# Memory attention and gated MLP: two issue loops and a hand-placed start replaced by one list of steps with named PSUM banks

## The chip, the cores and the metric

The kernel runs on one core of one Trainium2 chip. The metric is the device time of one execution in microseconds (us). The core has five instruction queues that run side by side and each in its own order: TensorE (PE, with its weight loads as PEld), VectorE (DVE), ScalarE (ACT), GpSimd (POOL) and SyncE (SP, which here issues every DMA). They wait for each other through semaphores. SBUF is the on-chip memory that all work on, PSUM the 8 banks of 128 x 512 float32 into which PE writes.

## The reference, cut to what matters

```python
B, H, S, D = (4, 8, 576, 64)
scores = scale * np.matmul(q, k.transpose(0, 1, 3, 2))      # causal mask, softmax over the last axis: a
local = np.matmul(a, v)
q_p = phi(q)                                                 # where(x > 0, x, exp(x) - 1) + 1
mem_ret = np.einsum('bhsd,bhde->bhse', q_p, M_prev)
mem_norm = np.einsum('bhsd,bhd->bhs', q_p, z_prev)[..., None] + 1e-06
x = g * mem_ret / mem_norm + (1 - g) * local                 # g = sigmoid(beta), one per head
x = x.transpose(0, 2, 1, 3).reshape(2304, 512)
out = ((x @ w_a) * (x @ w_b)) @ w_out                        # d_ff = 1536; weights are float64
```

## The kernel before, in words

**Attention.** Two heads of one batch are worked together as a pair, so there are 16 pairs. For each pair PE transposes keys and queries (steps `TK`, `TQ`, and `Tq` for the 64 rows of the tail), ACT copies them to SBUF (`th…`) and DVE makes what the copy rounded off (`tl…`), since every product is made of three products of high and low parts. PE adds the mask (`b_…`) and the scores (`S_…`), DVE takes the minima of the negated scores (`m…`), ACT the exponentials (`e…`), DVE the reciprocals of the sums (`r_`), POOL multiplies the probabilities by them (`n0` to `n4`), PE transposes them (`G…`), ACT and DVE copy them (`h…`, `l…`, group 0 by POOL with `w_`, `l0`), and PE multiplies by the values (`V…`). The result of a pair goes to DRAM (`st_`) and comes back for the memory part (`pa` to `py`), which for the first two blocks of tokens runs inside the attention too. The tail's scores (`S_4`) and the values' product (`V…`) use one PSUM tile of two banks in turn; the six other banks are handed out by `psum()` in rotation.

**What sets the order.** The table `ORDER` names each step once with a lag. A loop over 19 rounds issues in each round the steps of the table in that order, each for pair (round minus lag). Ahead of it the first loads, the mask, the identity matrix and 17 products of zeros on PE (`warm(17)`) are written out by hand; 12 more products of zeros, the zeroing of the memory matrices and the gates stand after round 0. POOL's first work is written as: zero both `qdiag` tiles, scale the first one after its load (`sq(0)`), then make the identity.

**MLP.** The tokens are six blocks t of 384, d_ff is twelve parts f of 128. A column is one (t, f): twelve products with w_a (called A here), twelve with w_b (B), then ACT copies B out of PSUM (`cx`, L852), DVE multiplies it by A (`mx`, L855), ACT rounds that (`hh`, L859) and DVE takes the rest (`hl`), and nine products with w_out add it into the output's banks (`outer`, L877). `column(t, f)` issues A, B, the four steps, and then `outer` of the column before. In the first 18 columns A and B take their banks from a pool of two. The column order is: t = 0 and 1 in turn for f = 0 to 5, then t = 0 for f = 6 to 11, then t = 1, then blocks 2 to 5.

**Weights.** They come as float64 and are turned into float32 by whole-number steps, in 24 units, two for each f: a large one (w_a and w_b, 1024 columns) and a small one (w_out, 512). A unit goes through `mag` (ACT, L760), `clamp` (POOL, L766), `shift`, `high`, `low` (DVE, L773, L780, L787), `hi` (ACT, L802) and `lo` (DVE). The first three units start inside the attention; the generator `conversion()` does the others, one or two behind each column by the table `UNITS`.

**Memory part of blocks 2 to 5.** `memory_unit` has the steps load, phi, norm, turn, retrieve (PE, L1012, into one PSUM bank) and join (DVE, L1019, then ACT and DVE for the halves). The tables `E2` and `R2` say at which column those of block 2 stand; `retrieve` is issued between A and B of its column, for block 2 twice in one column at the end (`R2 = (20, 21, 23, 23)`).

## Time and profile before

| what | value |
|---|---|
| median of three runs | 698.15 us (696.22 to 699.35) |
| the profiled execution, its time | 697.51 us |
| the profiled execution, span from first to last instruction | 695.6 us |
| PE busy | 669.8 us (96%) |
| DVE, ACT, POOL busy | 446.8, 319.4, 243.9 us |
| mean granted clock of TensorE | 0.993 |

The profiled execution lies 0.64 us under the median. Its time is 1.9 us longer than its span, which is what lies around the instructions. A busy share is an average over stages: the attention fills about the first 200 us, the columns with the weight conversion reach to about 330 us, and from 380 us on PE runs columns alone.

### The profile page before, as it was taken

What the parts mean: (1) busy time and instruction counts of PE and PEld (TensorE: products, weight loads), DVE (VectorE), ACT (ScalarE), POOL (GpSimd) and SP (SyncE); (2) the same over time, 40 slices, a digit from 0 to 9 for tenths busy, and PEclk for the clock granted to TensorE, in tenths of its full rate; (3) what the DMA queues carried; (4) which work ended last, traced back from release to release, by engine and by line L of the source; (5) the groups of instructions that cost most, each with busy time, mean ns of one, the idle gap of its engine ahead of it and who ended that gap; (6) DMA issues with size and microseconds to landing.
All of it is one profiled execution on the core that took longest, in us unless ns stands there. A gap on an engine that the chain in (4) does not pass through costs nothing.

```text
span 695.6 us, 11360 instructions
## 1 busy us (share of the span) xinstructions
PE 669.8 (96%) x4125; PEld 615.8 (89%) x4125; DVE 446.8 (64%) x901; ACT 319.4 (46%) x765; POOL 243.9 (35%) x354
## 2 busy tenths in 40 slices
PE   7999999999979999989988999999999999999997
PEld 6798888999879898878988999999999999999996
DVE  4999998988878887887776544545445545421111
ACT  2999999999875445443322322222212321221111
POOL 4699999999893232232501100001000000000000
PEclk9999999999999999999999999999999999999999
DMA  8666647456733435441413311112110400010001
GB/s 169 143 146 170 155 125 206 118 150 198 248 135 129 158 121 164 156 134 17 124 40 69 92 34 29 33 51 64 35 35 0 112 15 23 1 46 1 0 1 45
DMA packets 124663, 64.24 MB, mean 92 GB/s; under 512 B 97856, under 2 KB 116288, under 8 KB 124608
## 3 DMA queue, kind: packets, MB, share of 16 engines
q1 hardware_dynamic: 124608, 63.53, 33.7%
q8 instruction: 32, 0.52, 0.3%
q14 instruction: 23, 0.19, 0.1%
HBM read 49.35 MB, written 14.16 MB: 91 GB/s over the span
## 4 chain that ended last, share of the span: by engine, by line
PE 77%; DVE 13%; ACT 4%; issue 3%; DMA 1%; SPq 1%; POOL 0%; ACTq 0%; DVEq 0%; POOLq 0%
PE pp L840 35%; PE o L877 17%; PE pt L87 8%; PE pt L442 6%; PE pw L611 6%; DVE wt L787 2%; DVE wt L780 2%; ACT wh L802 2%; PE pw L442 2%; PE m L1012 1%; DVE PT L91 1%; DVE wt L773 1%; DVE x L855 1%; DVE nm L481 1%; DVE wl L91 1%
## 5 line engine op out<-in xcount | busy, mean ns | idle before, releaser
L840 PE MATMUL pp<-xh,wh 128*128 128x384 f32 x568 | 193.6, 341 | 6.7 <-ACT x L852 3.9
L840 PE MATMUL pp<-xh,wl 128*128 128x384 f32 x568 | 192.1, 338 | 0.6 <-DVE wl L91 0.6
L840 PE MATMUL pp<-xl,wh 128*128 128x384 f32 x568 | 191.6, 337 | 0.0
L840 PEld LDWEIGHTS pp<-xh,wh 128*128 128x128 f32 x568 | 107.5, 189 | 13.4 <-ACT x L852 6.7
L855 DVE TENSOR_TENSOR x<-pp,x 128x384 f32<-128x384 f32 x71 | 39.4, 555 | 124.0 <-ACT x L852 124.0
L840 PEld LDWEIGHTS pp<-xl,wh 128*128 128x128 f32 x568 | 107.7, 190 | 2.8
L840 PEld LDWEIGHTS pp<-xh,wl 128*128 128x128 f32 x568 | 107.5, 189 | 1.0 <-DVE wl L91 1.0
L852 ACT ACTIVATE x<-pp 128x384 f32<-128x384 f32 x71 | 34.5, 487 | 146.1 <-PE pp L840 146.1
L1004 POOL TENSOR_TENSOR xx<-xx 128x384 f32<-128x384 f32 x16 | 16.5, 1036 | 204.1 <-DMA xx<-xs 199.0
L511 POOL TENSOR_SCALAR P<-P,sum 128x128 f32<-128x128 f32 (+2 forms) x144 | 82.8, 596 | 12.1 <-DVE sum L503 9.6
L877 PE MATMUL o<-wh,hl 128*128 128x512 f32 x216 | 85.5, 396 | 0.0
L877 PE MATMUL o<-wl,hh 128*128 128x512 f32 x216 | 85.0, 393 | 0.0
L877 PE MATMUL o<-wh,hh 128*128 128x512 f32 x216 | 84.9, 393 | 0.0
L492 ACT ACTIVATE P<-pt,nm 128x512 f32<-128x512 f32 (+3 forms) x128 | 66.6, 531 | 6.3 <-DVE nm L481 5.8
L91 DVE TENSOR_TENSOR PT<-pt,PT 128x512 fp32r<-128x512 f32 (+2 forms) x112 | 61.7, 587 | 10.0 <-ACT PT L566 7.8
L91 DVE TENSOR_TENSOR hl<-x,hh 128x384 fp32r<-128x384 f32 x71 | 40.5, 571 | 42.0 <-ACT hh L859 42.0
L859 ACT ACTIVATE hh<-x 128x384 fp32r<-128x384 f32 x72 | 37.8, 525 | 62.3 <-DVE x L855 62.3
L611 PE MATMUL pw<-PT,vh 128*128 128x320 f32 (+4 forms) x416 | 61.4, 293 | 3.0 <-issue 2.2
L611 PEld LDWEIGHTS pw<-PT,vh 128*128 128x128 f32 x416 | 57.1, 189 | 5.3 <-POOL xh L249 2.4
L481 DVE TENSOR_REDUCE nm<-pt 128x1 f32<-128x512 f32 (+3 forms) x128 | 56.3, 482 | 8.4 <-PE pt L442 8.2
L766 POOL TENSOR_SCALAR wt<-wt 128x512 f32<-128x512 f32 (+1 forms) x21 | 30.2, 1439 | 74.3 <-ACT wt L760 74.2
L87 PE MATMUL pt<-ident,P 128*128 128x128 f32 (+1 forms) x400 | 52.4, 279 | 1.5 <-POOL P L511 1.2
(126 smaller groups left out, 1079.8 us busy)
## 6 DMA issues: line engine op xcount, KB each, us to landing
xs<-xo SPq DMA_DIRECT2D x16, 576.0 KB, 4.3
xx<-xs SPq DMA_DIRECT2D x48, 192.0 KB, 3.4
wr<-in_moe_w_a_dram SPq DMA_DIRECT2D x12, 512.0 KB, 3.7
wr<-in_moe_w_b_dram SPq DMA_DIRECT2D x12, 512.0 KB, 4.8
wr<-in_moe_w_out_dram SPq DMA_DIRECT2D x12, 512.0 KB, 3.3
out_dram<-ob SPq DMA_DIRECT2D x18, 256.0 KB, 2.1
qr<-in_q_dram SPq DMA_DIRECT2D x34, 128.0 KB, 3.5
kr<-in_k_dram SPq DMA_DIRECT2D x32, 128.0 KB, 4.1
```

What stands on the lines that cost most here:

```text
L87: nc.tensor.transpose(out, x, ident[0:x.shape[0], 0:x.shape[0]])
L91: eng.tensor_tensor(out=lo, in0=x, in1=hi, op=ALU.subtract)
L442: nc.tensor.matmul(o, lhsT=w, rhs=x, start=first, stop=True, skip_group_check=True)
L481: nc.vector.tensor_reduce(out=s["nm"][:, c:c + 1], in_=src, axis=AX.X, op=ALU.min)
L492: nc.scalar.activation(out=s["P", i][:, h, :], in_=src, func=AF.Exp, scale=-1.0, bias=s["nm"][:, c:c + 1], accum_out=s["sum"][:, c:c + 1],)
L511: nc.gpsimd.tensor_scalar(out=pr[:, h, :], in0=pr[:, h, :], scalar1=r[:, c:c + 1], scalar2=1.0, op0=ALU.mult, op1=ALU.mult,)
L611: nc.tensor.matmul(pv[:, a:hi], lhsT=w, rhs=x, start=(n == 0), stop=(n == len(ops) - 1))
L840: nc.tensor.matmul(pp, lhsT=w[:, w0:w0 + P], rhs=x[:, kk, :], start=(c == 0), stop=(c == 3 * KK - 1),)
L852: nc.scalar.activation(out=x, in_=ps[1], func=AF.Copy)
L855: nc.vector.tensor_tensor(out=h[0], in0=ps[0], in1=h[0], op=ALU.mult)
L859: nc.scalar.activation(out=h[1], in_=h[0], func=AF.Copy)
L877: nc.tensor.matmul(po[t, m], lhsT=hx[:, m * P:(m + 1) * P], rhs=w[:, w0:w0 + DM], start=(f == 0 and n == 0), stop=(f == NFT - 1 and n == 2),)
```

## The change

The loop over `ORDER`, the text ahead of it, `conversion()` with `UNITS`, and the first 30 columns with their memory units are replaced by one list. `schedule()` yields a name and a pair (or column, or unit) at a time: `HEAD` and `TAIL` are written out step by step, `LOOP` holds two tables with lags for the rounds 3 to 8 and 9 to 13. Steps that were one are now several: the four steps of a column, its A (`uA`) and B (`uB`), its `outer` (`uo`) and the writing of finished outputs (`ua`, `ub`, `uc`) each have a name; so has every step of a weight unit (`Kload`, `Kmag`, … `Klo`), the load of a unit, and the memory unit's steps, with phi, norm, turn and join cut into two or three. What each step computes is unchanged. The attention's six PSUM banks are no longer handed out in rotation: each `psum()` takes the next number of a list, `BANKS`. Columns 30 to 71 and their memory units keep the old loop.

```diff
-ORDER = """
-clamp0:2 h3A:3 b_3:1 hi1:4 l3A:3 pd:2 S_3:1 pe:3 m3B:1 e4:2 v_l:2 TK:0 TQ:0 mc:1 m3A:1 mag2:3
...
+HEAD = """
+Dk.0 id.0 zi.0 ib.0 wm.17 wm.12 TK.0 Dq.0 Dk.1 TQ.0 zq.0 zq.1 thK.0 thQ.0 mk.0 Ek.1 TK.1 thK.1 b_2.0
...
+BANKS = """
+0123450123453140253102432540324015324103502313502143501234253134251034215305431305412305143240313240
...
+LOOP = """
+H1:2 hh:4 pd:2 pe:3 shift1:3 TQ:0 py:4 h3A:3 me:3 clamp1:3 l3A:3 mx:3 e4:2 LM:2 b_3:1 thQ:0 px:4
...
+TAIL = """
+h3A.11 pe.11 pf.11 b_3.13 pb.12 S_3.13 l3A.11 v_l.12 TK.14 m3B.13 e4.12 px.10 e3B.13 m3A.13 fw.0
...
+def schedule():
...
+    yield from named(HEAD)
+    lags = {}
+    for k, text in enumerate(LOOP.split("/")):
+        names = [w.partition(":") for w in text.split()]
+        lags |= {nm: int(o) for nm, _, o in names if o}
+        for i in range(SPAN[k], SPAN[k + 1]):
+            for nm, *_ in names:
+                if i >= lags[nm]:
+                    yield nm, i - lags[nm]
+    yield from named(TAIL)
...
-        ps_t = late.enter_context(tc.tile_pool(name="ps_t", bufs=6, space=bass.MemoryType.PSUM))
+        ps_t = late.enter_context(tc.tile_pool(name="ps_t", bufs=1, space=bass.MemoryType.PSUM))
...
+        banks = iter("".join(BANKS.split()))
+
         def psum():
-            return ps_t.tile([P, 512], F32, tag="T", name="pt")
+            return ps_t.tile([P, 512], F32, tag="T" + next(banks), name="pt")
...
-        for i in range(NPAIR + max(lags.values())):
-            for nm, o in lags.items():
-                p = i - o
-                if nm in KINDS or 0 <= p < NPAIR:
-                    step[nm](p)
-                if p == NPAIR - 1 and nm in after:
-                    after[nm]()
-            if i == 0:
-                warm(12)
-                memory_store(mem)
-                gates()
+        step |= beyond
+        for nm, p in schedule():
+            step[nm](p)
...
+    def hidden(c, n):
+        t, f = columns[c]
+        key, tag = "ab", "ab"
...
+        cols[c][0][n] = half(t, f, n, pools[key].tile([P, DM], F32, tag=tag, name="pp"))
+
+    def done(c):
+        t, f = columns[c]
+        outer(t, f, cols[c][1][1:])
...
+            "uA": lambda c: hidden(c, 0),
+            "uB": lambda c: hidden(c, 1),
+            "uo": done,
...
+        for c in range(CUT, len(columns)):
+            column(c, lambda: memory(c, True))
```

**The start.** These are POOL's first instructions behind its constants, before and then after. `qdiag` is the tile that holds the queries' tail rows, `ident` the matrix against which PE transposes, `mask_f` the causal mask.

```order
L277 MEMSET qdiag_101 128x512
L277 MEMSET qdiag_102 128x512
L358 ISA
L358 TENSOR_SCALAR qdiag_101<-qdiag_101 128x512
masks.py:197 MEMSET ident 128x128
masks.py:199 AFFINE_SELECT ident<-ident 128x128
masks.py:29 MEMSET mask_f 128x128
```

```order
masks.py:197 MEMSET ident 128x128
masks.py:199 ISA
masks.py:199 AFFINE_SELECT ident<-ident 128x128
L739 MEMSET qdiag_101 128x512
L739 MEMSET qdiag_102 128x512
masks.py:29 MEMSET mask_f 128x128
masks.py:30 AFFINE_SELECT mask_f<-mask_f 128x128
L451 TENSOR_SCALAR qdiag_101<-qdiag_101 128x512
```

The identity moves from behind the scaling of `qdiag`, which waits for a load, to POOL's first place. PE's first instructions, again before and then after (`idle` is the tile of zeros, `kr` and `qr` are keys and queries, `f` their transposed halves):

```order
L294 MATMUL pt<-idle 128x256 x17
L87 MATMUL pt<-ident,kr 128x128 x4
L87 MATMUL pt<-ident,qr 128x128 x4
L87 MATMUL pt<-ident,kt 128x128
L87 MATMUL pt<-ident,qdiag_101 128x128
L294 MATMUL pt<-idle 128x256 x12
```

```order
L387 MATMUL pt<-idle 128x256 x29
L187 MATMUL pt<-ident,kr 128x128 x4
L187 MATMUL pt<-ident,qr 128x128 x4
L187 MATMUL pt<-ident,kr 128x128 x4
L535 LDWEIGHTS ident_b
```

The second group of products of zeros now stands ahead of the first transposes, and the keys of the second pair are transposed before the first scores.

**The conversion beside the columns.** These are ACT's instructions at the columns 12 and 13, before and then after. `x<-pp` is a column's `cx`, `hh<-x` its `hh`, `wh<-wt` a weight unit's `hi`, `wt<-wr` its `mag`.

```order
L852 ACTIVATE x<-pp 128x384
L859 ACTIVATE hh<-x 128x384
L802 ACTIVATE wh_4409<-wt 128x512
L760 ACTIVATE wt<-wr 128x512
L802 ACTIVATE wh_4474<-wt 128x1024
L760 ACTIVATE wt<-wr 128x1024
L852 ACTIVATE x<-pp 128x384
L859 ACTIVATE hh<-x 128x384
```

```order
L921 ACTIVATE x<-pp 128x384
L928 ACTIVATE hh<-x 128x384
L893 ACTIVATE wh_4408<-wt 128x512
L853 ACTIVATE wt<-wr 128x512
L921 ACTIVATE x<-pp 128x384
L893 ACTIVATE wh_4489<-wt 128x1024
L853 ACTIVATE wt<-wr 128x1024
L928 ACTIVATE hh<-x 128x384
```

The copy of column 13 stood behind two units' steps and now stands behind one; the large unit's two steps come after it.

**The memory units of block 2.** These are DVE's instructions around the first `join`, before and then after. `xx<-m` is the join, which empties the bank of a `retrieve`; the rows ahead of it are phi and norm of a later unit, `q<-ph` with STREAM_TRANSPOSE is a turn.

```order
L966 TENSOR_SCALAR ph<-ph 128x384
L969 SCALAR_TENSOR_TENSOR ph<-q_4870,ph 128x384
L977 TENSOR_TENSOR q_4870<-ph,z_4703 128x384
L985 TENSOR_REDUCE n_4931<-q_4870 128x12
L988 COPY n_4933<-n_4931 32x12 x4
L989 TENSOR_TENSOR n_4932<-n_4931,n_4933 128x12
L990 TENSOR_SCALAR n_4932<-n_4932,over_gate_64 128x12
L994 RECIPROCAL n_4932<-n_4932 128x12
L995 TENSOR_TENSOR ph<-ph,n_4932 128x384
L1019 TENSOR_TENSOR xx<-m,xx 128x384
L91 TENSOR_TENSOR xl_69<-xx,xh_68 128x384
L855 TENSOR_TENSOR x<-pp,x 128x384
```

```order
L1079 RECIPROCAL n_4896<-n_4896 128x12
L1084 TENSOR_TENSOR ph<-ph,n_4896 128x384
L1115 TENSOR_TENSOR xx<-m,xx 128x384
L191 TENSOR_TENSOR hl<-x,hh 128x384
L1090 STREAM_TRANSPOSE q_4826<-ph 128x384
L924 TENSOR_TENSOR x<-pp,x 128x384
L1049 TENSOR_SCALAR ph<-ph 128x384
L1052 SCALAR_TENSOR_TENSOR ph<-q_4834,ph 128x384
L191 TENSOR_TENSOR xl_69<-xx,xh_68 128x384
```

Before, the join of unit 0 stands behind phi and norm of unit 2; now it stands ahead of them, behind those of unit 1. On PE there were B of column 20, an `outer` and A of column 21 between the `retrieve` of unit 0 and that of unit 1; now B of the columns 20 and 21, A of column 20 and an `outer` stand there, and the last two units' `retrieve`, which followed each other in one column, have an A between them. From column 4 on `outer` also stands a column later than it did: A and B of column 4 follow those of column 3 with no `outer` between them, `outer` of column 2 comes behind them, and so on until two of them stand behind column 14.

## Rows read from the trace of the kernel before

**Rows 1.** Busy time by stage: stretch, PE, PEld, DVE, ACT, POOL, clock.

```profile
40.00:180.00 140.00, 139.84 (x1216) 124.94 (x1216) 128.82 (x281) 129.38 (x373) 132.77 (x214) 1.00 0.62 161
180.00:217.48 37.48, 32.43 (x259) 30.36 (x258) 31.76 (x60) 27.34 (x71) 29.35 (x44) 1.00 0.45 152
217.48:327.82 110.34, 104.37 (x528) 94.81 (x528) 87.84 (x116) 51.55 (x76) 32.55 (x24) 0.98 0.42 136
327.82:380.00 52.18, 47.61 (x240) 44.13 (x241) 39.10 (x83) 13.83 (x28) 11.03 (x14) 0.97 0.32 76
```

**Rows 2.** The same view of the three stretches at half clock.

```profile
24.50:27.80 3.30, 3.30 (x23) 3.08 (x22) 3.22 (x8) 3.12 (x13) 3.30 (x6) 0.50 0.94 207
...
307.90:311.10 3.20, 3.20 (x11) 3.20 (x11) 3.13 (x5) 1.12 (x2) 1.24 (x1) 0.50 0.43 155
359.10:362.30 3.20, 3.20 (x11) 3.20 (x12) 2.08 (x4) 1.29 (x4) 0.00 (x0) 0.50 0.29 69
```

**Rows 3.** Start, in order of time: start, duration, instruction, idle time before it.

```profile
1.19 4.00 PE L294 MATMUL pt<-idle 128*128 128x256 f32 x17 [1.19 <-DVE idle L283]
...
7.16 0.62 POOL L358 TENSOR_SCALAR qdiag<-qdiag 128x512 f32<-128x512 f32 x1 [5.44 <-DMA qdiag<-in_q_dram]
...
8.35 1.12 PE L87 MATMUL pt<-ident,kr 128*128 128x128 f32 x4 [3.17 <-POOL ident masks.py:199]
...
10.40 2.91 PE L294 MATMUL pt<-idle 128*128 128x256 f32 x12
...
13.48 0.80 PE L442 MATMUL pt<-f 64*128 64x512 f32 x2
```

**Rows 4.** PE's longest wait while the pipeline fills, in order of time.

```profile
23.91 0.38 PE L442 MATMUL pt<-mask,ident_b 128*128 128x128 bf16 x4 [1.73 <-ACT P L492]
```

**Rows 5.** PE at the end of the attention, in order of time.

```profile
200.23 1.83 PE L611 MATMUL pw<-PT,vh 128*128 128x256 f32 x13 [2.23 <-issue]
...
205.86 3.35 PE L87 MATMUL pt<-ident,P 128*128 128x128 f32 x25 [1.20 <-POOL P L511]
```

**Rows 6.** ACT ahead of the first of these waits.

```profile
197.74 1.18 ACT L760 ACTIVATE wt<-wr 128x1024 f32<-128x1024 f32 x1
...
199.25 0.79 ACT L492 ACTIVATE P<-pw,nm 128x576 f32<-128x576 f32 x1
```

**Rows 7.** The chain that ended last, around column 14: start, duration, work.

```profile
305.02 1.14 ACT wt L760
...
306.58 6.00 PE pp L840 x24
312.59 2.09 PE o L877 x9
314.68 4.19 PE pp L840 x24
```

**Rows 8.** PE's first product of columns 12 and 14, in order of time.

```profile
289.65 0.44 PE L840 MATMUL pp<-xh,wh 128*128 128x384 f32 x1 [0.67 <-ACT x L852]
...
306.58 0.44 PE L840 MATMUL pp<-xh,wh 128*128 128x384 f32 x1 [3.28 <-ACT x L852]
```

**Rows 9.** Groups by form, 217 to 328 us: busy, mean ns, idle before.

```profile
L91 DVE TENSOR_TENSOR hl<-x,hh 128x384 fp32r<-128x384 f32 x16 | 8.9, 559 | 9.5 <-ACT hh L859 9.5
```

**Rows 10.** The weight units' tile, 217 to 330 us: POOL's clamp, ns min/median/max.

```profile
L766 POOL TENSOR_SCALAR wt<-wt x21: 616/1442/1546, 219.7 to 322.6; 128x512 f32<-128x512 f32 x11, 128x1024 f32<-128x1024 f32 x10
```

**Rows 11.** The memory units of block 2, in order of time.

```profile
358.23 0.55 DVE L1019 TENSOR_TENSOR xx<-m,xx 128x384 f32<-128x384 f32 x1
...
358.92 0.60 PE L1012 MATMUL m<-yh,md 128*128 128x384 f32 x1 [2.16 <-DVE xx L1019]
...
376.10 0.41 PE L1012 MATMUL m<-yh,md 128*128 128x384 f32 x1 [1.76 <-DVE xx L1019]
```

**Rows 12.** The chain through the first of them.

```profile
358.92 1.24 PE m L1012 x3
360.16 3.18 PE pp L840 x12
```

More of the change, by code (lines that the diff above doesn't have):

```diff
@@ L99, in evac @@
         split_lo(nc.vector, lo, src, hi, scale)
-    def run(gen, n):
-        return any(next(gen, "end") == "end" for _ in range(n))
     mid = ctx.enter_context(tc.tile_pool(name="mid", bufs=1))
@@ L258, in memory_pair, with attention @@
         return {f.__name__: f for f in (Lp, pa, pb, pc, pd, pe, pf, px, py)}
-    def attention(late, early, tiles, after, more):
+    def attention(late, early, tiles, after, more, beyond):
         raw = late.enter_context(tc.tile_pool(name="raw", bufs=2))
@@ L909, in column @@
+    def column(c, between):
+        hidden(c, 0)
         between()
-        hidden(1)
-        for go in product(ps, HLE[t > 1], h):
-            go()
-        if pend:
-            outer(*pend.pop())
-        pend.append((t, f, h[1:]))
+        hidden(c, 1)
+        for go in cols[c][2]:
+            go()
+        done(c - 1)
+        t, f = columns[c - 1]
+        if f == NFT - 1:
+            for m in range(TPB):
+                written(t, m)
+    UNIT = (
+        "load phi phi2 norm norm2 norm3 turn turn_h turn_l sums retrieve join join_h join_l"
+    )
@@ L1028, with unit_step @@
     columns += [(t, f) for t in range(2, NB) for f in range(NFT)]
-    plan, units = {}, {}
-    for t in range(2, NB):
+    plan, units, made = {}, {}, set()
+    for t in range(3, NB):
         for j in range(KK):
-            c = E2[j] if t == 2 else (t - 1) * NFT + 3 * j
-            rr = R2[j] - c if t == 2 else 2
-            early = ((-2, "load"), (-1, "phi norm"), (0, "turn"))
-            late = ((-1, "load"), (0, "phi norm turn"))
-            for o, names in (*(early if t == 2 else late), (rr, "retrieve join")):
-                plan.setdefault((c + o, o == rr), []).extend((t, j, nm) for nm in names.split())
-    def memory(c, mid):
+            c = (t - 1) * NFT + 3 * j
+            late = (
+                (-1, "load"),
+                (0, "phi phi2 norm norm2 norm3 turn turn_h turn_l sums"),
+                (2, "retrieve join join_h join_l"),
+            )
+            for o, names in late:
+                plan.setdefault((c + o, o == 2), []).extend((t, j, nm) for nm in names.split())
+    def unit_step(t, j, nm):
         def psum():
@@ L1094 @@
-        attention(late, early, tiles, {"TK": first_weights, "S_4": turn_over}, more)
-        first.close()
-        late.close()
-        pool(mlp_r, "ab", "right", 2, space=bass.MemoryType.PSUM)
-        pool(mlp_l, "w")
-        pool(mlp_l, "o", space=bass.MemoryType.PSUM)
-        pool(second, "o1", space=bass.MemoryType.PSUM)
-        chunks = conversion(does)
-        run(chunks, UNITS[0])
-        for t, h in enumerate(begun):
-            if pend:
-                outer(*pend.pop())
-            pend.append((t, 0, h[1:]))
@@ L1133, with over @@
-        outer(*pend.pop())
+        cols[0] = {}, []
+        for n in range(2):
+            more[f"H{n}"] = lambda psum, n=n: cols[0][0].update({n: half(0, 0, n, psum())})
+        for nm, go in zip(("cx", "mx", "hh", "hl"), product(*cols[0][:1], nc.gpsimd, cols[0][1])):
+            more[nm] = lambda _, go=go: go()
+        def over():
+            first.close()
+            late.close()
+            pool(mlp_r, "ab", "right", 2, space=bass.MemoryType.PSUM)
+            pool(mlp_l, "w")
+            pool(mlp_l, "o", space=bass.MemoryType.PSUM)
+            pool(second, "o1", space=bass.MemoryType.PSUM)
@@ new lines @@
+        for m, nm in enumerate(("ua", "ub", "uc")):
+            beyond[nm] = lambda c, m=m: written(columns[c][0], m)
+        for nm in ("load", "mag", "clamp", "shift", "high", "low", "hi", "lo"):
+            beyond["K" + nm] = does[nm]
+        for nm in UNIT.split():
+            beyond["q_" + nm] = lambda n, nm=nm: unit_step(2 + n // KK, n % KK, nm)
+        attention(late, early, tiles, {"TK": first_weights, "S_4": turn_over}, more, beyond)
+        for c in range(CUT, len(columns)):
+            column(c, lambda: memory(c, True))
+            memory(c, False)
@@ L1134 @@
+        done(len(columns) - 1)
+        for m in range(TPB):
+            written(NB - 1, m)
         mlp_r.close()
```

293 lines of the change are left out of this document (183 added, 110 removed).

## The prediction, as it was put on record

> **What bounds the kernel now.** I read the busy time by stage first, then PE's own waits, then the chain that ended last, and for each long wait the instructions ahead of the one that PE waited for. By stage PE is the bound nearly everywhere: from 40 to 180 us, where the attention runs in its steady state, it is busy 139.84 of 140 us [rows 1], so no order of the same instructions can win anything there. DVE, ACT and POOL are close behind (128.82, 129.38 and 132.77 of 140), so something can be lost there. From 380 us on the columns follow each other without a gap that the waits of PE show. What can be won lies in the four places between: the start, the hand-over from attention to columns (32.43 of 37.48 us busy), the columns that run beside the weight conversion (104.37 of 110.34) and those beside the memory units of block 2 (47.61 of 52.18) [rows 1].
>
> A second loss does not show as idle time. In three stretches the granted clock is 0.50, the lower of the two levels (1.2 instead of 2.4 GHz) [rows 2]; PE is busy through all of each. The first begins behind a wait of 1.73 us, the second behind one of 3.28 us, the third at the end of one of 2.16 us [rows 4, 8, 11]. In the second, 24 products of a column take 6.00 us where 24 others take 4.19 [rows 7].
>
> **The change part by part.** No instruction of the computation is added or removed; all of it is order, and the finer names only make other orders possible. The sum goes against the profiled execution, 697.5 us, which is 0.6 us under the median.
>
> The start. PE's first transposes wait 3.17 us for the identity, which POOL makes after a scaling that itself waited 5.44 us for a load [rows 3]. Then 12 products of zeros (2.91 us) stand between these transposes and the first scores, which begin at 13.48 us. Afterwards the identity is POOL's first work, and all 29 products of zeros run in one piece ahead of the transposes: from 1.19 us on they take at most 4.00 + 2.91 = 6.9 us, so the transposes begin near 8.1 us instead of 8.35. From there to the first scores it is 5.13 us now; without the 12 products it is 2.2 us if nothing else were in the way, and 5.1 if the copies and low parts on ACT and DVE take all of it. I put the first scores at 11.2 us, 2.3 us earlier, nearer to the short end since ACT's and DVE's order begins with the steps that these scores need. Behind it the pipeline fills, with a wait of 1.73 us for an exponential [rows 4] and a stretch at half clock that costs PE half of 3.30 us, 1.65 us [rows 2]. ACT is busy there for 3.12 of 3.30 us, so the fill goes at ACT's pace whatever PE's order is; of these 3.4 us I count 0.7. Together 3.0 us, between 0 and 0.25 + 2.9 + 3.4 = 6.5.
>
> The attention's rounds. The tables keep the lags and nearly the order on PE. I count 0. There is no room for a gain (0.16 us idle in 140). The unknown cost is the list of banks: a step now waits for the reader of one named bank. Its bound from below is 0, from above the one bank wait of this kind in the trace, 1.73 us [rows 4], in each of 16 pairs; as six banks still serve in turn and PE's order in a round is nearly kept, I take the lower end, with up to 4 us (0.25 us a pair) inside the range and the rest as a rival.
>
> The hand-over. PE is idle 37.48 - 32.43 = 5.05 us in it [rows 1]. Of that 2.23 us stand ahead of the last pair but one's product with the values, and 1.20 us ahead of the last pair's transposes, which wait for POOL [rows 5]. In the first case the two-bank PSUM tile has to be emptied by an exponential, which stands on ACT behind a weight unit's 1.18 us [rows 6]. Afterwards that `mag` stands behind the exponential, and POOL's last additions of the memory part (`px`, `py`) stand behind the multiplications that the transposes wait for. But the same product now follows closely on the copies of its own last transposes, so that wait does not vanish. I count about half of it and most of the second: 2.2 us, between 0 and 5.05.
>
> The columns beside the conversion. Sixteen columns take 110.34 us [rows 1]; at 4.19 + 2.09 = 6.28 us each [rows 7] it would be 100.5. So 9.8 us are lost, and the largest piece is column 14: PE stood still 3.28 us [rows 8], since its bank was to be emptied by a copy that stood on ACT behind two units' steps, the last of them 1.14 us long [rows 7], and then ran 24 products in 6.00 instead of 4.19 us, 1.81 us more. In the new order that copy stands behind one unit instead of two. What can DVE give? It works 87.84 of the 110.34 us and is idle for 22.5. Of this idle time 9.5 us are waits for `hh`, since `hl` directly follows `mx` in each of the 16 columns [rows 9]; in the new order other steps stand between these two in 14 of 16 columns, which frees 9.5 x 14/16 = 8.3 us. If the rest of its waits stays, DVE's way through the stretch is 87.84 + 22.5 - 8.3 = 102.0 us, close above PE's 100.5. One new wait comes in: A of column 4 now follows directly on B of column 3 and needs a bank which the copy of B frees; the nearest row is that wait at 0.67 us [rows 8], paid once. Behind it `outer` runs a column later, and its own wait for `hh` and `hl` is covered by a whole column. So 102.7 us, a gain of 7.6, between 0 (DVE's idle time stays) and 9.8 - 0.7 = 9.1.
>
> Here the traces bear on a cost of the denser order. POOL's clamp takes 0.62 us at its shortest and 1.44 us in the middle [rows 10], though half of the 21 are only 512 wide: most of them are stretched by work beside them. The Trainium skill, SBUF — State Buffer, section "Who interferes with whom", has a rule that speaks against this change: DVE and GpSimd share a port pair as an exclusive lock, and a DVE instruction with two SBUF inputs makes a GpSimd instruction that reads SBUF wait for its whole length. By that rule the trace agrees (0.62 against 1.44), and a DVE without pauses would make more clamps late; by the rows, 0.82 us more on each of the 21 would be 17 us on POOL, which has 77.8 us free, but on the path of the units it can hold the conversion at its old pace, and that is the second case below.
>
> The memory units. PE waits 2.16 and 1.76 us for a join to empty the bank that the next `retrieve` needs [rows 11]; the first join stands on DVE behind phi and norm of a later unit. Behind the first wait the clock is halved: 12 products take 3.18 us [rows 12] where half of 4.19 is 2.10, and the three of the `retrieve` 1.24 us, about half of it for the clock, 1.7 us in all. Together 5.6 us. In the new order the join stands ahead of that unit's steps, and a B or an A more lies between two `retrieve`s: a product of 2.1 us covers a wait of 2.16 or 1.76, with the rest at most 0.1. I count 5.0 us, between 1 and 5.6.
>
> The sum is 3.0 + 0 + 2.2 + 7.6 + 5.0 = 17.8 us: 697.5 - 17.8 = 679.7, rounded to 680 us.
>
> **The rivals.** First, DVE binds the columns beside the conversion: its 22.5 us of idle time are waits inside a unit (a large one passes ACT, POOL, DVE, ACT, DVE in turn, in one buffer), and filling the gap before `hl` only moves them. What speaks for it: DVE has the highest share after PE there, and the stretched clamps [rows 10]; against it that units run ahead of their columns. The stage then gains 2 us instead of 7.6: 685.3 us.
>
> Second, no change that can be told: PE's waits move to other steps, because DVE, ACT and POOL are filled to 92 to 95% in the attention and the order that it leaves them in only shifts which of PE's instructions waits. For it speaks that the fill goes at ACT's pace; against it that three of the long waits come from one instruction standing ahead of another without need. Between 694.7 and 698.
>
> Third, slower: the listed banks make PE wait once in each pair of the attention. Its price is 1.73 us a pair as in the fill [rows 4]: 16 x 1.73 = 27.7, 679.7 + 27.7 = 707.4 us. It decides from 17.8/16 = 1.1 us a pair, where all gains are eaten. For it speaks that the rotation gave the bank that was used longest ago, and a list that is made for other durations than the chip's does not; against it that PE's order within a round hardly changes.
>
> **How the numbers follow.** I give the forecast case 0.66, DVE binding 0.17 (0.10 without the stretched clamps), no change 0.09, slower 0.08. A measurement of this kernel can tell about 0.5% (3.5 us) from no change. The first two cases are faster by more than that: 0.83; the third is within: 0.09; the last is slower: 0.08. The best ends of all terms together give 697.5 - (6.5 + 5.05 + 9.1 + 5.6) = 671.3 us, and 671 is the range's low end. Its high end of 696 takes in the second case and the lower part of the no-change case; above it are the slower rival and the rest of that case, some 0.12, and below 671 hardly anything. The likeliest case alone lies between 674 and 688.
>
> **What would show it.** First score products near 11.2 us, and no wait of PE for the identity. No PE wait above 1 us between 215 and 400 us, none of 0.7 us except at column 4, and no stretch at half clock there: the columns 1 to 16 in about 103 us. In the attention PE still idle under 0.5 us in 140. DVE busy near 86% of the stretch beside the conversion instead of 80%. If those 16 columns still take 108 us or more with DVE idle ahead of `hi` and `lo`, the first rival holds; if the rounds of the attention take longer than now and PE waits there for readers of banks, the third. The prediction is wrong above all if the waits of the new order add up where I see none: at the named banks.

## The result, and the profile after

The changed kernel takes 675.81 us (median of 4, 674.57 to 676.11), the kernel before in the same comparison 697.86 us (696.22 to 699.35). The ratio is 0.9681, with a 95% interval of 0.9656 to 0.9707: faster by 22 us, and 4 us faster than forecast. The profiled execution took 676.11 us (before 697.51), its span is 674.3 us. PE is now busy 98% of it and its mean granted clock is 1.000 (0.993 before).

The page of the kernel after, part 1:

```profile
PE 660.1 (98%) x4125; PEld 609.8 (90%) x4125; DVE 440.0 (65%) x901; ACT 317.2 (47%) x765; POOL 236.8 (35%) x354
```

Busy time by stage of the kernel after (stretch, PE, PEld, DVE, ACT, POOL, clock), which answers to [rows 1]:

```profile
33.00:180.00 147.00, 144.89 (x1272) 131.71 (x1271) 134.16 (x295) 134.34 (x395) 138.48 (x224) 1.00 0.60 160
180.00:210.82 30.82, 27.33 (x212) 24.82 (x210) 28.14 (x49) 22.92 (x54) 25.82 (x36) 1.00 0.42 138
210.82:312.20 101.38, 100.80 (x528) 94.21 (x529) 87.71 (x117) 50.62 (x74) 24.43 (x24) 1.00 0.47 154
312.20:398.00 85.80, 85.33 (x448) 79.55 (x447) 54.66 (x128) 24.20 (x50) 15.67 (x20) 1.00 0.29 70
```

The reader is to see three things. In the two stages of columns hardly an idle microsecond is left to PE (0.58 of 101.38, 0.47 of 85.80), and the granted clock is 1.00 in every row. In the attention's rounds PE has more idle time than before, 2.11 of 147 us instead of 0.16 of 140. And the hand-over still has 3.49 idle of 30.82. This row begins at 180 us as before, which is by then a later place in the work; the marks below compare like with like.

The start of the kernel after, PE in order of time, against [rows 3]:

```profile
1.19 5.64 PE L387 MATMUL pt<-idle 128*128 128x256 f32 x29 [1.19 <-DVE idle L750]
6.66 0.60 PE L187 MATMUL pt<-ident,kr 128*128 128x128 f32 x4
...
8.44 0.44 PE L535 MATMUL pt<-f 64*128 64x384 f32 x2 [0.19 <-ACT f L511]
...
22.81 0.85 PE L187 MATMUL pt<-ident,P 128*128 128x128 f32 x6 [0.60 <-ACT P L585]
...
27.04 0.62 PE L704 MATMUL pw<-PT,vh 128*128 128x256 f32 x3
```

No wait for the identity; four transposes take 0.60 us instead of 1.12; the longest wait of the fill is 0.60 us instead of 1.73 [rows 4]. The last row is the first product with the values. It makes a good mark for the end of the fill: it stands at 27.04 us, in the kernel before at 32.66.

With such marks the 21.4 us can be laid out for every kernel of this study. Each column is a stage in us, taken from the starts of PE's instructions: the first score product, the first product with the values, twelve pairs of rounds from there, the hand-over up to A of column 1, columns 1 to 16, columns 17 to 29, and the rest.

| kernel | time, us | ratio to before (95%) | first scores at | first values at | 12 pairs | hand-over | col. 1-16 | col. 17-29 | rest |
|---|---|---|---|---|---|---|---|---|---|
| before | 697.86 | | 13.48 | 32.66 | 143.80 | 41.02 | 110.34 | 91.84 | 275.96 |
| after | 675.81 | 0.9681 (0.9656-0.9707) | 8.44 | 27.04 | 142.77 | 41.00 | 101.39 | 85.80 | 276.25 |
| b_start | 697.75 | 0.9991 (0.9970-1.0013) | 8.33 | 33.23 | 143.58 | 40.94 | 110.37 | 91.72 | 275.96 |
| b_ma | 701.50 | 1.0040 (1.0019-1.0062) | 13.39 | 31.61 | 146.75 | 41.15 | 111.52 | 91.79 | 275.95 |
| b_start_ma | 702.12 | 1.0035 (1.0013-1.0056) | 8.47 | 32.38 | 146.69 | 42.20 | 111.45 | 91.88 | 275.97 |
| b_mask | 708.22 | 1.0132 (1.0097-1.0167) | 13.48 | 34.84 | 150.60 | 41.45 | 110.37 | 91.84 | 275.95 |
| b_conv | 696.57 | 0.9978 (0.9951-1.0006) | 13.29 | 32.30 | 143.57 | 41.95 | 109.37 | 91.49 | 275.96 |
| b_conv2 | 694.57 | 0.9930 (0.9905-0.9955) | 13.57 | 34.33 | 143.95 | 40.95 | 105.18 | 92.90 | 275.95 |
| b_units | 698.37 | 0.9990 (0.9964-1.0016) | 12.55 | 33.79 | 143.55 | 40.94 | 110.34 | 92.15 | 275.95 |
| b_units2 | 699.53 | 1.0012 (0.9988-1.0035) | 13.32 | 35.33 | 143.61 | 40.95 | 108.78 | 94.32 | 275.96 |
| a_rot | 675.80 | 0.9685 (0.9648-0.9722) | 8.73 | 27.39 | 142.63 | 40.80 | 101.37 | 85.82 | 276.25 |
| a_split | 675.99 | 0.9678 (0.9646-0.9711) | 9.00 | 27.41 | 142.67 | 40.81 | 101.37 | 85.82 | 276.26 |
| a_hl | 684.66 | 0.9799 (0.9760-0.9838) | 9.02 | 27.62 | 143.25 | 41.80 | 110.20 | 85.04 | 276.26 |
| a_outer | 677.66 | 0.9704 (0.9671-0.9736) | 8.66 | 27.35 | 142.74 | 40.50 | 104.02 | 85.01 | 276.24 |

b_ kernels are the kernel before with one or two parts of the change, or something near them, a_ kernels the kernel after with one part undone. Each ratio is against runs of the kernel before taken beside that kernel, with medians of 697.86 to 699.60 us, so it can't be had from the column of times alone. The stages come from one profiled execution each, so two rows that share a stage's code show how much it varies: with before's start 32.30 to 35.33 us to the first values (five traces), with after's 27.04 to 27.62. By these the trace of the kernel before lies near the low end, and the gain of the start could be put up to 8 us. The gain of 21.4 us is 5.62 + 1.03 + 0.02 + 8.95 + 6.04 - 0.29. One thing blurs the second and third of these: seven of PE's transposes (four of keys, three of the memory tiles) stand ahead of the mark at the end of the twelve pairs in the kernel before and behind it in the kernel after. From start to start they take 0.8 us in the one and 0.9 in the other, so with the same work on each side the twelve pairs gain about 0.2 us and the hand-over about 0.8.

### The profile page after: what moved, and what is told of

It reads as the page before. It is cut to its first block, busy times and chain, and to the rows that moved or that the text cites. A ratio compares the mean times of both kernels' runs of the same rounds, so it can differ in the third digit from the quotient of the medians.

```text
span 674.3 us, 11381 instructions
## 1 busy us (share of the span) xinstructions
PE 660.1 (98%) x4125; PEld 609.8 (90%) x4125; DVE 440.0 (65%) x901; ACT 317.2 (47%) x765; POOL 236.8 (35%) x354
## 4 chain that ended last, share of the span: by engine, by line
PE 79%; DVE 15%; POOL 3%; ACT 2%; issue 1%; ACTq 0%; DVEq 0%; POOLq 0%
PE pp L909 43%; PE o L946 22%; DVE nm L574 4%; PE pt L187 4%; DVE PT L191 4%; PE pw L704 4%; PE pt L535 3%; POOL P L604 1%; PE m L1108 1%; DVE f L191 1%; PE pw L535 1%; PE pt L387 1%; DVE f L193 1%; DVE sum L593 1%; PE pt L909 1%
## 5 line engine op out<-in xcount | busy, mean ns | idle before, releaser
L909 PE MATMUL pp<-xh,wh 128*128 128x384 f32 x568 | 191.5, 337 | 1.8 <-ACT x L921 0.9
L604 POOL TENSOR_SCALAR P<-P,sum 128x128 f32<-128x128 f32 (+3 forms) x144 | 81.4, 585 | 7.0 <-DVE sum L596 7.0
L585 ACT ACTIVATE P<-pt,nm 128x128 f32<-128x128 f32 (+3 forms) x128 | 67.1, 532 | 11.3 <-DVE nm L574 10.2
L191 DVE TENSOR_TENSOR hl<-x,hh 128x384 fp32r<-128x384 f32 x71 | 42.0, 591 | 27.8 <-ACT hh L928 27.6
L574 DVE TENSOR_REDUCE nm<-pt 128x1 f32<-128x128 f32 (+3 forms) x128 | 55.6, 479 | 5.3 <-PE pt L535 5.0
L659 ACT ACTIVATE PT<-pt 128x512 fp32r<-128x512 f32 (+2 forms) x112 | 52.1, 527 | 2.6 <-PE pw L704 2.0
```

Of the source, the lines that this page charges most:

```text
L191: eng.tensor_tensor(out=lo, in0=x, in1=hi, op=ALU.subtract)
L574: nc.vector.tensor_reduce(out=s["nm"][:, c:c + 1], in_=src, axis=AX.X, op=ALU.min)
L585: nc.scalar.activation(out=s["P", i][:, h, :], in_=src, func=AF.Exp, scale=-1.0, bias=s["nm"][:, c:c + 1], accum_out=s["sum"][:, c:c + 1],)
L604: nc.gpsimd.tensor_scalar(out=pr[:, h, :], in0=pr[:, h, :], scalar1=r[:, c:c + 1], scalar2=1.0, op0=ALU.mult, op1=ALU.mult,)
L659: nc.scalar.activation(out=dst, in_=src, func=AF.Copy)
L909: nc.tensor.matmul(pp, lhsT=w[:, w0:w0 + P], rhs=x[:, kk, :], start=(c == 0), stop=(c == 3 * KK - 1),)
```

## The experiments

**The start.** b_start takes the identity, the masks and all products of zeros to the front:

```diff
         load_pair(0, "kq")
+        mask = p2_e.tile([P, P], BF16, name="mask", bufs=1)
...
+        make_identity(nc, ident)
+        nc.vector.tensor_copy(ident_b, ident)
+        make_causal_mask(nc, mask_f, mask_val=FAR)
...
         warm(17)
+        warm(12)
         load_tails(0, "k")
...
             if i == 0:
-                warm(12)
                 memory_store(mem)
```

> The kernel before with the start alone of the change: the identity and the masks are made ahead of POOL's scaling, and all 29 products of zeros stand in one piece ahead of the first transposes. First theory, the whole gain of the start comes from these two: the first score product stands at 9 to 11 us instead of 13.48, no wait of TensorE for the identity is left, and the first product with the values (32.66 us before, 27.04 after the change) comes 3 to 5.6 us earlier, the whole time by as much. Second theory, the fill goes at ACT's pace: the scores begin earlier, but the first product with the values moves by 2 us at most, since the order behind it is the old one.

The scores begin at 8.33 us, as in the kernel after, and nothing is gained: the first values' product stands at 33.23 us. Timelines of b_start, SP's queue, ACT and PE:

```profile
17.81 0.60 SPq L145 DMA_DIRECT2D qr<-in_q_dram  x1
```

```profile
22.08 0.63 ACT L171 ACTIVATE ph<-qr 128x512 f32<-128x512 f32 x1 [4.92 <-DMA qr<-in_q_dram]
```

```profile
23.91 0.37 PE L442 MATMUL pt<-mask,ident_b 128*128 128x128 bf16 x2 [6.19 <-ACT P L492]
```

ACT stands still for 4.92 us with `ma` of the first memory tile at its head, whose load SP issued at 17.81 us; behind it wait the exponentials that empty PE's banks. The granted clock is 0.50 from 21.4 to 28.1 us, a stretch twice as long as in the kernel before [rows 2]. The second theory holds in its outcome and falls in its reason: here the fill doesn't go at ACT's pace but at this load's. In the kernel before the row stands at the same 22.08 us, with 0.46 us of waiting ahead of it; in b_units, which has the same start, it stands at 23.22 us behind 2.86 us. The kernel after issues that load earlier, and ACT finds it there:

```profile
13.17 0.51 SPq L240 DMA_DIRECT2D qr<-in_q_dram  x1
```

```profile
19.21 0.66 ACT L266 ACTIVATE ph<-qr 128x512 f32<-128x512 f32 x1
```

b_ma and b_start_ma take ACT's step away from the head instead:

```diff
-ma:0 b_2:1 H0:3 thK:0 pc:2 r_:2 mb:0 px:4 ...
+b_2:1 H0:3 thK:0 pc:2 r_:2 px:4 ...
...
-... n2:2 low1:3 mu:0
+... n2:2 low1:3 ma:0 mb:0 mu:0
```

> The kernel before, with one thing moved: ma and mb, the exponential and the feature steps of the memory tile, which wait for a load, are issued later in each round, directly ahead of mu, behind the exponentials of the scores. Nothing of the start is changed. In the run of the start alone the first score product stood 5.2 us earlier, and ACT then waited 4.92 us for this very load, which landed at 22.08 us as in the kernel before (where ACT waited 0.46 us for it). First theory, the load at the head of ACT's queue sets the fill: TensorE's wait of 1.73 us and the half clock behind it go, and the first product with the values comes 1.5 to 3.5 us earlier than 32.66. Rival, something else holds the fill: less than 0.7 us.

> The run of the start alone, with ma and mb moved as well, as in the run beside it. First theory, the gain of the start needs both, scores that begin early and an ACT that doesn't stand waiting for the memory tile's load: TensorE's wait of 6.2 us goes, the first product with the values stands at 27 to 29 us instead of 33.23, and the time falls by 4 to 6 us. Rival, the fill is held by more than this load: it stays above 31 us, the time within 2 us of before.

Alone, the move does what the theory says at its place, in a smaller size than the 1.5 to 3.5 us expected: ACT doesn't wait for the load, PE's wait falls from 1.73 to 0.65 us, the clock stays at 1.00 from 20 to 33 us, and the first values' product comes at 31.61 us, 1.05 us earlier than in the kernel before and 0.7 us below the lowest trace with the old start. The rounds lose more: 146.75 us; the loss lies in the first four pairs (12.2 us each instead of 11.5), and its cause stays open. With the early start the move isn't enough. ACT runs a copy and an exponential ahead of the step now, then waits 3.00 us for the load up to 21.79 us, and PE waits for the next exponential behind it; b_start_ma, PE:

```profile
23.14 0.48 PE L87 MATMUL pt<-ident,kt 128*128 128x128 f32 x1 [3.03 <-ACT P L492]
```

By these rows the early scores need the early load too. No run moved that load, so that it is needed and that it suffices is argued, not shown. a_split puts 12 products of zeros back behind the first transposes of the kernel after:

```diff
-Dk.0 id.0 zi.0 ib.0 wm.17 wm.12 TK.0 Dq.0 ... TK.1 thK.1 b_2.0
+Dk.0 id.0 zi.0 ib.0 wm.17 TK.0 Dq.0 ... TK.1 thK.1 wm.12 b_2.0
```

> The kernel after, with the 12 products of zeros back behind the transposes of the first steps, ahead of the first mask products; the identity stays POOL's first work. First theory, the early identity carries the start: the first score product stands within 1.5 us of 8.44, the time within 1.5 us of 675.8. Rival, it is the products of zeros in one piece: the clock is still at half during the transposes (1.12 us for four instead of 0.60), the 12 products stand ahead of the scores, which begin at 10.5 us or later, and the first product with the values comes 2 to 4 us later, the whole time with it.

The first theory holds: scores at 9.00 us, the same time. PE of a_split:

```profile
4.98 1.05 PE L187 MATMUL pt<-ident,kr 128*128 128x128 f32 x4
...
7.26 1.68 PE L387 MATMUL pt<-idle 128*128 128x256 f32 x12
```

The first transposes are slow again (1.05 us), but they begin 1.68 us earlier, and the 12 products take 1.68 us instead of the 2.91 of the kernel before [rows 3]. The products' place is worth nothing in time. That the early identity carries the early scores is what is left by this; no run put the identity alone back.

**The banks.** a_rot takes the six banks in rotation again:

```diff
-ps_t", bufs=1, ...    tag="T" + next(banks)
+ps_t", bufs=6, ...    tag="T"
```

> The kernel after, with its six PSUM banks taken in rotation instead of by the list; every engine's order is the same, instruction for instruction. First theory, the list as such is worth nothing, since the rotation gives the bank that was asked for longest ago: within 1.5 us of 675.8. Rival, the finer order needs the list, because some readers come much later than the rotation assumes: several waits of 0.5 to 1.8 us for banks in the rounds, and 4 us or more slower.

675.80 us and the same stages: the list is worth nothing in this order, and it costs nothing. In the rounds the one long wait for DVE is there in both (1.1 us with rotation, 1.2 with the list).

**The rounds.** b_mask moves one word of the order table:

```diff
-V1A:3 Lv:0 pb:2 V2A:3 ... px:4 S_2:1 shift1:3 shift0:2 b_:1 S_:1
+V1A:3 Lv:0 pb:2 b_:1 V2A:3 ... px:4 S_2:1 shift1:3 shift0:2 S_:1
```

> The kernel before, with the mask products of the rounds' largest score group (b_) issued ahead of the second pair of value products, so that in each round the score products of the two groups follow each other without mask products between them. The rounds after the change took 12.05 us a pair instead of 12.25, with no idle time of TensorE to be saved. First theory, the score products with 64-row operands cost less when no other shape stands between their groups: the rounds take about 0.2 us a pair less, 2 to 3 us in all. Rival, the place of the mask products has nothing to do with it: the same time within 1 us.

Neither time comes out: the rounds grow by 6.8 us. What the first theory says of the products does hold. The smallest score products, by form (busy, mean ns, idle before), in the rounds of before, b_mask and after:

```profile
L442 PE MATMUL pt<-f 64*128 64x128 f32 x22 | 3.6, 323 | 0.0
```

```profile
L436 PE MATMUL pt<-f 64*128 64x128 f32 x22 | 2.5, 220 | 0.0
```

```profile
L535 PE MATMUL pt<-f 64*128 64x128 f32 x22 | 2.5, 219 | 0.0
```

The same 22 products (those of eleven pairs) take 0.10 us less each when no mask product stands right ahead of them, and b_mask reaches the row of after with this one edit. These durations overlap. What PE gains by it is read from each product's start to the next one's: over twelve pairs the 24 of this form take 0.72 us instead of 1.96, and the 48 products 64x384 ahead of them 4.19 instead of 5.30 (after 4.17), together 2.4 us or 0.2 us a pair. But mask products that come earlier take their banks earlier, which in this order are not yet empty; waits of b_mask's PE in the rounds:

```profile
PE pt L436 <- ACT P L486: 3.2, 6, 0.9
PE pt L436 <- DVE nl L85: 1.8, 5, 0.4
```

Twelve pairs take 150.60 us instead of 143.80. These waits are 5.0 us of the loss. With pauses too short for this view PE is idle for 5.80 us in all, and PE is busy 144.80 us instead of 143.64 although the score products got cheaper; where that went I can't assign. So a wait for a bank has a price, but 0.4 us a pair and not the 1.73 of the third rival. The kernel after has the cheap products without these waits; which of its moves avoids them wasn't tried.

**The columns beside the conversion.** b_conv fills DVE's gap ahead of `hl`:

```diff
-        for go in product(ps, HLE[t > 1], h):
-            go()
+        cx, mx, hh, hl = product(ps, HLE[t > 1], h)
+        cx()
+        run(chunks, 1)
+        mx()
+        hh()
+        run(chunks, 1)
+        hl()
```

where the steps of a unit now stop ahead of `hi` and ahead of `lo`.

> The kernel before, with one thing of the conversion's columns moved: the first copy of a weight unit (hi) stands on ACT between a column's cx and hh, and its low part (lo) on DVE between that column's mx and hl, instead of both behind hl. Nothing else is moved, and A, B and outer keep their order. First theory, DVE's waits ahead of hl (9.5 us over 16 columns) are what the stretch loses: they fall below 3 us, the columns 1 to 16 go from 110.34 to 101 to 104 us, and the time falls by 6 to 9 us. Rival, DVE's idle time only moves to another wait inside the units: the stretch gains 2 us at most.

The gap is gone, but the stage still takes 109.37 us. Groups of b_conv's DVE in columns 1 to 16 (busy, mean ns, idle before):

```profile
L787 DVE SCALAR_TENSOR_TENSOR wt<-wr,wt 128x512 uint32<-128x512 uint32 (+1 forms) x20 | 25.8, 1289 | 0.7
L91 DVE TENSOR_TENSOR wl<-wt,wh 128x512 fp32r<-128x512 f32 (+1 forms) x22 | 21.2, 964 | 11.2 <-ACT wh L802 11.1
...
L859 DVE TENSOR_TENSOR x<-pp,x 128x384 f32<-128x384 f32 x16 | 8.8, 551 | 4.5 <-ACT x L856 4.4
L91 DVE TENSOR_TENSOR hl<-x,hh 128x384 fp32r<-128x384 f32 x15 | 8.3, 551 | 0.0
```

Of 9.5 us [rows 9], 2.8 go into waits ahead of `lo` (8.4 before), 1.3 ahead of `mx` (3.2 before), 4.4 into longer instructions (DVE is busy 92.24 us instead of 87.84), and 1.0 is what the stage gains. One operation, `low` of the small units, grows by 5.8 us, and the others together shrink by 1.4: it now starts while POOL clamps, where in the kernel before it started just ahead of the clamp. DVE and POOL in order of time, in before and in b_conv:

```profile
254.00 0.69 DVE L787 SCALAR_TENSOR_TENSOR wt<-wr,wt 128x512 uint32<-128x512 uint32 x1
254.18 1.41 POOL L766 TENSOR_SCALAR wt<-wt 128x1024 f32<-128x1024 f32 x1 [5.59 <-ACT wt L760]
```

```profile
253.42 1.16 POOL L766 TENSOR_SCALAR wt<-wt 128x1024 f32<-128x1024 f32 x1 [5.96 <-ACT wt L760]
253.71 1.41 DVE L787 SCALAR_TENSOR_TENSOR wt<-wr,wt 128x512 uint32<-128x512 uint32 x1
```

DVE's operation takes 1.41 us at 8 of the 10 places of this form; in the kernel before it took 0.69 us at all 10, and the clamp beside it was the long one. So the rival holds for this edit alone, with nearly half of the price from a cause that it didn't name. And PE still waits 3.28 us in column 14, behind the copy of column 13 [rows 8]. b_conv2 also issues the second unit of a two-unit column behind the next column's `cx` and `mx`:

```diff
+        if extra:
+            extra.pop()
+            run(chunks, 2)
+            cx()
+            mx()
+            run(chunks, 1)
+            hh()
+            run(chunks, 1)
+            hl()
+            run(chunks, 1)
+        else:
...
+            if c in (2, 7, 10, 12):
+                extra.append(c)
```

> The run with hi and lo between a column's steps, and one thing more: after the columns 2, 7, 10 and 12 the second weight unit is issued behind the next column's cx and mx instead of ahead of them. In the first run DVE no longer waited ahead of hl, but TensorE still waited 3.28 us in column 14, for a copy on ACT that stood behind two units, and the clock fell behind it. First theory, the columns need both: that wait and the half clock (1.81 us) go too, the columns 1 to 16 take 102 to 105 us instead of 110.34, and the time falls by 5 to 8 us. Rival, the copy is late because DVE is: the wait moves to mx or to another column, and the stretch stays above 108 us.

Stage of b_conv2:

```profile
219.23:324.41 105.18, 102.10 (x528) 93.59 (x529) 90.33 (x115) 50.80 (x76) 25.06 (x24) 1.00 0.42 141
```

105.18 us, no wait above 0.93 us, the clock at 1.00, and the time falls by 0.7%. The two moves together gain 5.2 us in the stage, the first alone 1.0. The second alone wasn't run: the wait in column 14 and the slower column behind it, 3.28 + 1.81 = 5.1 us, are nearly all of it, so that both were needed isn't shown by these two. Two experiments on the kernel after show what the rest of the new order does. a_hl puts `hh` and `hl` back behind `mx` in columns 6 to 14 (in column 13 only closer to it):

```diff
-umx.6 uhh.6 Kshift.10 uB.7 Khigh.10 uo.5 Klo.9 Klow.10 uA.8 uhl.6
+umx.6 uhh.6 uhl.6 Kshift.10 uB.7 Khigh.10 uo.5 Klo.9 Klow.10 uA.8
```

> The kernel after, with hh and hl issued directly behind mx in columns 6 to 14, as the kernel before does in all; TensorE's order is untouched. First theory, what the conversion's columns gained is DVE's time ahead of hl: DVE waits about 0.6 us again in each of the 9 columns, 5.4 us in all, and the stretch, in which TensorE and DVE are filled to 99 and 87%, loses 3 to 5 us. Rival, the gain comes from the place of outer and of the copies, and DVE has room: less than 1 us lost.

a_hl, the stage and the row of `hl`; then the kernel after, the same row:

```profile
212.67:322.87 110.20, 103.69 (x529) 93.43 (x529) 87.65 (x115) 49.62 (x74) 24.53 (x24) 1.00 0.42 141
```

```profile
L191 DVE TENSOR_TENSOR hl<-x,hh 128x384 fp32r<-128x384 f32 x15 | 9.8, 654 | 9.9 <-ACT hh L928 9.9
```

```profile
L191 DVE TENSOR_TENSOR hl<-x,hh 128x384 fp32r<-128x384 f32 x15 | 9.6, 642 | 1.6 <-ACT hh L928 1.6
```

All of the stage's gain is gone (110.20 us), though PE's order is untouched. DVE's idle time ahead of `hl` grew by 8.3 us and the stage by 8.8: by that I read DVE's chain, busy 87.65 us plus its waits, as what sets the pace; PE's waits, 6.5 us, are for the copies and products behind it. `hh` moved on ACT as well, and the two weren't separated. The size was twice what I expected, since I took PE's slack to absorb some. a_outer issues `outer` of columns 2 to 13 earlier again, as soon as the next column's B and its own `hl` are listed:

```diff
-uA.8 uhl.6 Khi.10 Kmag.11 Klo.10 ucx.7 ... uB.8 Kshift.11 Khigh.11 Kmag.12 uo.6
+uA.8 uhl.6 uo.6 Khi.10 Kmag.11 Klo.10 ucx.7 ... uB.8 Kshift.11 Khigh.11 Kmag.12
```

> The kernel after, with outer of columns 2 to 13 issued on TensorE a step or two earlier, directly behind the next column's B, where the kernel before has it. First theory, its later place is what lets hh and hl come late without a cost: TensorE waits for hl or hh in most of the 12 columns, 0.2 to 0.5 us each, and the time rises by 3 to 5 us. Rival, hl is done in time anyway: less than 1 us.

The stage loses 2.6 us and 0.8 come back behind it: 1.85 us in the median. PE doesn't wait for `hl` but for `cx` (1.8 us in three waits): the later `outer` is time for ACT's copies. The loss lies between the theory's 3 to 5 us and the rival's 1, and the wait was not the one expected.

**The memory units.** b_units moves two numbers, b_units2 the second of them (`E2`) alone. Both belong to the third unit, number 2 counted from 0:

```diff
-    R2 = (20, 21, 23, 23)
+    R2 = (20, 21, 22, 23)
-    E2 = (18, 19, 20, 22)
+    E2 = (18, 19, 21, 22)
```

> The kernel before, with the second memory unit of block 2 begun a column later and the third retrieved a column earlier, so that a join no longer stands behind the next units' phi and norm. First theory, TensorE's waits of 2.16 and 1.76 us and the half clock behind the first (1.7 us) go: 4 to 6 us less. Rival, the waits move to another retrieve or to the columns' copies: 0 to 2 us less.

> The kernel before, with the second memory unit's successor begun a column later and every retrieve where it was. In the first run of this kind TensorE's two waits for joins had gone, but a third retrieve a column earlier waited 3.0 us for ACT, right behind its own turn. First theory, the first wait of 2.16 us and its half clock (1.7 us) go and the second of 1.76 stays: 3 to 4 us less. Rival, the later phi and norm make the second wait longer by what the first gave: within 1 us of before.

Neither gains. PE's waits in columns 17 to 29 of b_units, then of b_units2:

```profile
PE m L1012 <- ACT yh L98: 3.0, 1, 3.0
```

```profile
PE m L1012 <- DVE xx L1019: 5.7, 1, 5.7
```

In b_units both waits for joins [rows 11] are gone, and the third `retrieve` waits for its own `turn`, which stands right ahead of it; around this wait the granted clock is 0.50 from 366.8 to 373.6 us. In b_units2 the later phi and norm stand ahead of the third unit's join, and one wait of 5.7 us takes the place of two. Neither of these two places for whole steps avoids both waits; others weren't tried. The kernel after cuts phi, norm, turn and join into 12 pieces (turn alone into four) and has no such wait; from column 1 to column 30 these two rows, the second of them ahead of A of column 1, are all of PE's waits that the view lists:

```profile
PE pp L909 <- ACT x L921: 0.9, 2, 0.6
PE pp L909 <- ACT xo L713: 0.7, 1, 0.7
```

Which of the cuts carries it, or the changed order of PE's own steps, wasn't separated.

No kernel of the study is measurably faster than the change as it is.

## Why the prediction was right, term by term

| term | forecast, us | measured, us |
|---|---|---|
| start and fill | 3.0 (0 to 6.5) | 5.6 |
| rounds | 0 (-4 to 0) | 1.0 |
| hand-over | 2.2 (0 to 5.05) | 0.0 |
| columns beside the conversion | 7.6 (0 to 9.1) | 9.0 |
| memory units | 5.0 (1 to 5.6) | 6.0 |
| rest | 0 | -0.3 |
| sum | 17.8 | 21.4 |

**Start.** Mis-sized, and right in part by luck. Of the 5.6 us, 5.04 lie ahead of the first scores (8.44 instead of 13.48 us; the forecast had 2.3) and 0.58 in the fill behind them (18.60 instead of 19.18 us; the forecast had 0.7). The scores beat the forecast of 11.2 by 2.8 us: the products of zeros took 5.64 us where the sum put up to 6.9, so that the transposes began at 6.66 instead of 8.1, and from there to the scores it was 1.78 us where the sum put 3.1. The luck lies in what followed. The forecast let the earlier scores count in full at the end of the fill without asking what the fill waits for, and b_start shows that in the old order they count for nothing. "The fill goes at ACT's pace whatever PE's order is" was read from ACT's busy share in one stretch of 3.3 us, which began behind ACT's own wait; the row that counts stood just ahead of it, ACT waiting for a load (0.46 us in the kernel before, 4.92 in b_start). The change also issues this load at 13.17 us instead of 18.82, which the prediction doesn't name. I followed PE's wait one step back, to an exponential, and not two.

**Rounds.** Near 0 in the sum, not in the parts. PE is busy 140.86 us in the twelve pairs instead of 143.64 and idle 1.91 instead of 0.16, where the forecast wanted under 0.5; 1.17 of that stand in one wait (below). "No room for a gain" took the instructions' durations as given, and the order changes them: about 2.4 us come from the score products that b_mask shows. The seven transposes that moved behind the mark are another 0.8 us and no gain.

**Hand-over.** Mis-sized. `mag` no longer stands ahead of the exponential, and the wait of 2.23 us [rows 5] is gone, but in its place PE waits 1.12 us for a multiplication on POOL and 0.46 and 0.47 us in two other places, and the 0.74 us ahead of column 1 is as before. From mark to mark PE's idle time fell from 5.05 to 3.69 us and its busy time rose from 35.97 to 37.32, the seven transposes among it. So the stage is as long as before, and about 0.8 us is what it gained for the same work.

**Columns beside the conversion.** The mechanism held and its size was 1.4 us short: DVE's share is 86.5% as forecast, the 16 columns take 101.4 us where the sum gave 102.7, the wait in column 4 is 0.58 us where it put 0.67. DVE's idle time fell from 22.5 to 13.7 us, 7.9 of that ahead of `hl`, where the sum took 8.3; a_hl gives it back. The reason given was half the story: in the old order freeing DVE ahead of `hl` gains 1.0 us while the copies still stand late (b_conv), and the two together 5.2 us (b_conv2).

The stretched clamps went the other way than feared. After, by form:

```profile
L859 POOL TENSOR_SCALAR wt<-wt 128x1024 f32<-128x1024 f32 x10 | 11.8, 1183 | 35.5 <-ACT wt L853 35.5
L859 POOL TENSOR_SCALAR wt<-wt 128x512 f32<-128x512 f32 x11 | 10.1, 917 | 43.2 <-ACT wt L853 43.2
```

The 512-wide ones take 0.92 us at a mean, the 1024-wide 1.18, where the kernel before has 1.45 and 1.43. The rows of before and b_conv above show the two ways: where DVE began 0.18 us ahead, the clamp took 1.41 us and DVE 0.69; where the clamp began 0.29 us ahead, it took 1.16 and DVE 1.41. The section of the Trainium skill on the shared ports (SBUF — State Buffer, "Who interferes with whom") says that issue order decides which engine waits; by that the traces agree. The prediction used the rule in one direction only.

**Memory units.** Right in place and near in size: the waits were 5.6 us, and 6.0 are gained. That moving a unit by a column does not do it (b_units, b_units2) the prediction didn't say; that the gain hangs on the finer steps is argued from these two, not shown.

**The rivals.** DVE binding describes the two runs that lack one part of the new order in these columns, b_conv (1.0 us gained in the stage) and a_hl (0.1 us left of the gain); it doesn't hold for the whole. That waits only move, the second rival, is what b_start, b_units and b_units2 show, each for its part. The third rival was wrong as to the list (a_rot); a bank taken too early does cost (b_mask), at a quarter of the price that the rival gave.

## What to carry to other kernels

When PE waits for an engine, follow that engine's own waits to the end before calling it full: in b_start two steps led from PE over an exponential to a load that was issued 17.8 us after the start. Parts of a schedule needn't add: of the parts tried alone on the old order none gained measurably and two lost, though the whole gains 22 us, so a part that shows nothing alone isn't worthless. When two stages are compared by marks, count the instructions on each side: seven transposes that crossed a mark looked like a gain of 0.8 us. And a gap that an order fills must be priced with what then runs side by side: in b_conv nearly half of what DVE won ahead of `hl` it lost to longer instructions, above all one that ran beside POOL's clamp.

## What the hardware showed that was not expected

A tiny DVE instruction can take ten times its time. In the rounds of the kernel after, POOL, DVE and PE in order of time:

```profile
85.29 1.28 POOL L277 TENSOR_TENSOR qr<-ph,zr 128x512 f32<-128x512 f32 x1
...
86.22 1.62 DVE L593 SCALAR_TENSOR_TENSOR sum<-sum,over_ungate 128x9 f32<-128x9 f32 x1
...
86.53 1.29 POOL L191 TENSOR_TENSOR vh<-vr,vh 128x512 fp32r<-128x512 f32 x1
...
88.69 0.22 PE L535 MATMUL pt<-mask,ident_b 128*128 128x128 bf16 x1 [1.17 <-DVE f L193]
```

Nine columns take 1.62 us here, against 0.16 us at the shortest of its 16 executions, and end at 87.84 us, within 0.02 us of the second POOL operation's end (87.82). Behind it on DVE stands what PE waits for. In the kernel before the longest of the 16 takes 1.28 us, so it isn't the new order's alone. That POOL holds DVE up is read from these times; no run moved the one away from the other.

The half clock behind a wait isn't certain. PE waits 3.3 us ahead of column 14 in before, b_conv and b_units2; the stretch's mean clock is 0.98 in the first two and 1.00 in the third. b_units2 has the code of the kernel before in this stretch, and the stretch is 1.6 us shorter there (108.78 us).
